# Decode steps in another order: three a slot in the later slots, words first in a step, two tiny loads issued first

## The chip, the cores and the metric

The kernel runs on one core of one Trainium2 chip. The metric is device time in microseconds (us) of one execution. Three executions of the kernel before took 1134.91, 1138.04 and 1139.94 us; the median is 1138.04 us. The profiled execution took 1136.57 us, of which 1134.7 us lie between its first and its last instruction.

## The reference

An attention block feeds two expert blocks, all in float32:

```
scores = q @ k^T / sqrt(64) + bias(distance, head), kept on the last 96 keys and the first 8
x  = softmax(scores) @ v                 # 4 x 8 heads x 768 x 64  ->  3072 x 512
h  = ((x @ w1) * (x @ w2)) @ w3          # 512 -> 1024
x2 = h @ w_out                           # 1024 -> 512
h2 = x2 @ w_in                           # 512 -> 2048
out = (h2 * cos(h2)) @ w_out2            # 2048 -> 512
```

`n_local` (96) and `n_global` (8) come as 64-bit integers, and the weights come as 64-bit words, so that each weight has to be decoded into float32 on the chip before it can be used.

## The kernel before, in words

The work runs in three stretches on one instruction stream per engine; the order is written out by hand in the code, and each engine takes its instructions in that order.

**Decoding a weight.** A weight piece of 128x512 values is loaded as 512 KB of 64-bit words into a `raw` buffer (`w_load`, L325, on SyncE's queue, called SP). Then ScalarE (ACT) makes two conversions, the "words" (`dec_words`, L338 and L339), and VectorE (DVE) makes a shift (`dec_shift`, L343), a sign (`dec_sign`, L347) and a sum (`dec_sum`, L355; the sum reads `raw` for the last time). Pieces of w1 and w2 are then split into a high part by a cast on ACT (`w_hi`, L419) and a low part on DVE (`w_lo`, L423). Pieces of w_in make seven combinations each pair (`combos`), and pieces of w_out2 are stored to DRAM (`late_w`, L359) for later. The pieces stand in one list of 72: 16 of w3 and w_out in turn, 24 of w3, w1 and w2, 16 of w_in and 16 of w_out2. The generator `decoder()` goes through that list one piece a step and stops (`yield`) after nearly each DVE operation; `decode(n)` runs it on by n stops. So `decode` calls, spread over the code of the other work, set where decoding stands in each engine's queue. The first 30 pieces ("fast") use six raw buffers, the later ones three.

**Start and chunks.** The start issues the first loads, computes the bias tables (`biases`, from `n_local` and `n_global`, which ACT's queue loads into `nraw`), and then 16 chunks multiply w3 with w_out into W (`wmm`, L890, float32 products) while the first attention units run: scores (L582), maximum with bias (`a_max`, L610), exponential (`a_exp`, L621), normalizing (`a_norm`, L631, L634, then L640 on ACT or L642 on GpSimd), transposes (L649, L651), a copy of them (L659, L664), values (`a_values`, L676).

**Slots.** Then 8 x 12 slots follow. Each runs one attention unit, 14 units ahead, and 24 products of the first expert block in two halves of 12 (L432): in the first eight slots of twelve the products with w1 and w2 (`up`), in the last four the products with W (`down`), whose result a slot later goes through one buffer, x2t (`down_out` L748, one buffer; `down_store` L751). Every third slot starts with the values of three units, whose v tile was loaded one slot earlier (`a_load_v`, L551).

**Second block.** After the slots the second expert block runs from the stored pieces; it has no decoding.

SP's queue takes its DMAs in the order of the code. A load into a raw buffer waits there until the sum that last read this buffer is done, and everything behind it on SP waits too.

Of the kernel before, what the change touches and what calls it, by code (L numbers as in the profile page):

```python
# [269 lines left out]
def fused(ctx, tc, a_qk, a_v, w3p, wo1p, w1p, w2p, winp, wo2p, n_global, n_local, out):  # L270
# [269 lines left out]
    def a_load_plain(n, queue=None):  # L540

        if not 0 <= n < PLAIN:
            return
        t = plain[n] = attn.tile([128, QK_W], F32R, tag="hh", name="hh")[0:64].bitcast(F32)
        (queue or nc.sync).dma_start(out=t, in_=a_qk[n, 0:64])
# [235 lines left out]
    with tc.manual_schedule():  # L781
# [8 lines left out]
        for o in "3A3A3A3A3A3A3A3ABBBBBBBB":  # L790
# [3 lines left out]
            else:  # L794
                n, m = ups.pop(0)
# [7 lines left out]
        tp = pool("tp", 1, side="right")  # L803
        EARLY = 30
# [6 lines left out]
        def decoder():  # L811


            n = len(dec)
            for i in range(2):
                w_load(*dec[i][:2])
            for i in range(n + 5):
                fast = i < EARLY
                k = [dec[i - l][0] if 0 <= i - l < n else None for l in range(5)]

                def ready(stage, lag):

                    for l in range(4, lag - 1, -1):
                        if k[l] and (stage, k[l]) not in done:
                            done.add((stage, k[l]))
                            if stage == "sum" or k[l] in xs and isinstance(dest[k[l]], str):
                                yield k[l]

                if fast and i + 2 < EARLY:
                    w_load(*dec[i + 2][:2])  # L830
                if k[0] and fast:
                    dec_words(k[0])
                if k[1]:
                    dec_shift(k[1])
                    yield
                for key in ready("sum", 2):
                    dec_sum(key)
                    yield
                for key in ready("hi", 3 if fast else 2):
                    w_hi(key, dest[key])  # L840
                for key in ready("lo", 4 if fast else 2):
                    w_lo(key, nc.vector)
                    yield
                if k[1]:
                    dec_sign(k[1])
                    yield
                if not fast:
                    for key in ready("sum", 1):
                        dec_sum(key)
                        yield  # L850
                    if k[1] and k[1][0] == "in" and k[1][1] % 2:
                        yield from combos(k[1][1] // 2)
                if EARLY <= i + 2 < n:
                    w_load(*dec[i + 2][:2])
                if k[0] and not fast:
                    dec_words(k[0])

        dest = {key: d for key, _, d in dec}
        done = set()
# [3 lines left out]
        def decode(n):  # L863
            for _ in range(n):
                next(steps_left, None)

        a_load_plain(0, nc.scalar)
        a_scores(0)
        nc.vector.memset(pt_ps, 0.0)
        steps_b = biases(tp)  # L870
        next(steps_b)
        make_identity(nc, ident)
        nv = dists = None
        for i in range(21):
# [9 lines left out]
        for c, (h, k) in enumerate(chunks):  # L884
            n = c - 1 if c < 2 * M1 - 1 else -9
            if k == 0:
                W_ps = {m: p_mm.tile([128, 512], F32, tag="mm", name="mm") for m in range(4)}

            def wmm(m):
                nc.tensor.matmul(  # L890
                    W_ps[m], lhsT=wt["w3", c][:, m * 128:(m + 1) * 128], rhs=wt["wo1", k],
                    start=k == 0, stop=k == M1 - 1,
                )
                if k == M1 - 1:
                    t = wt["W", 4 * h + m] = wts.tile(
                        [128, 2, 512], F32R, tag="Wb" if h else "Wa", name="W", bufs=4
                    )
                    nc.scalar.copy(out=t[:, 0, :], in_=W_ps[m])
                    nc.vector.tensor_tensor(
                        out=t[:, 1, :], in0=W_ps[m], in1=t[:, 0, :].bitcast(F32), op=ALU.subtract  # L900
                    )

            a_load(n + 3)
            a_load_v(n + 1 if n >= 0 else -1)
            if c < 4:
                bias_heads(*dists, range(2 * c, 2 * c + 2))
            elif c == 4:
                tp.release()
            if n > 0:
                a_scores(n)  # L910
            if n >= 0:
                a_load_plain(n + 2)
            a_values(n - 2)
            a_max(n)
            if c == 2 * M1 - 1:
                for m in range(4):
                    wmm(m)
            decode(1)
            a_out(n - 2)
            a_split_hi(n + 2)  # L920
            a_exp(n)
            decode(1)
            a_split_lo(n + 2)
            if c < 2 * M1 - 1:
                wmm(0)
                wmm(1)
            if c in (2, 3):
                wmm(2)
                wmm(3)
            a_transpose(n - 1)  # L930
            a_tcopy(n - 1)
            a_norm(n, True, lambda: decode(1)) if n >= 0 else decode(2)
            decode(2 if c < 8 else {14: 1, 15: 5}.get(c, 3))
            if not (c in (2, 3) or c == 2 * M1 - 1):
                wmm(2)
                wmm(3)
# [18 lines left out]
        def stage_tile():  # L955
            return wts.tile([128, 2, TB2], F32, tag="wA", name="x2f")
# [52 lines left out]
        for j in range(NB1):  # L1009
            for i in range(UPB):  # L1010
                sl = j * UPB + i
                n = sl + LEAD
                last = j == NB1 - 1
                if last and i == 0:
                    attn.release()
                    x2cA = pool("x2cA", 1)
                    x2_pool.update({k: x2cA for k in ("B11", "T2", "T1", "T3", "B21", "B22")})
                a_load(n + 3)
                if last:
                    if i == 0:  # L1020
                        x2_loads(0)
                        late_load(0)
                    elif i == 1:
                        late_load(1)
                        r0, r1 = stage_tile(), stage_tile()
                        nc.sync.dma_start(out=r0, in_=x2_cols("B12", 0))
                        x2_now = x2_steps(r0, r1)
                    elif i == 2:
                        late_load(2)
                    elif 3 <= i < 9:  # L1030
                        piece_load(0, i - 3)
                    if i == 7:
                        late_load(3)
                    if 8 <= i:
                        late_store(i - 8)
                a_scores(n)
                a_load_plain(n + 2)
                if (n - 2) % TPB == TPB - 1:
                    for u in range(n - 1 - TPB, n - 1):
                        a_values(u)  # L1040
                if n > LEAD + 1:
                    a_load_v(n - 1)
                a_split_hi(n + 2)
                if 1 <= i <= M1:
                    up_mult(j, i - 1)
                    up_hi(j, i - 1)
                a_max(n)
                decode(2)
                if i == 0 and j > 0:
                    down_out(j - 1, MO - 1)  # L1050
                    down_store(j - 1, MO - 1)
                elif i > M1:
                    down_out(j, i - M1 - 1)
                    down_store(j, i - M1 - 1)
                if 1 <= i <= M1:
                    up_lo(j, i - 1)
                a_exp(n)
                a_out(n - 2)
                a_split_lo(n + 2)
                if i < M1:  # L1060
                    up(j, i, "a")
                    up_copy(j, i)
                else:
                    down(j, i - M1, 0)
                a_transpose(n - 1)
                a_tcopy(n - 1)
                a_norm(n, sl < 8)
                decode(2 if sl < 8 or sl >= 48 else 1)
                if last and 2 <= i < 10:
                    some(x2_now, 1)  # L1070
                if i < M1:
                    up(j, i, "b")
                else:
                    down(j, i - M1, 1)
                if last and 2 <= i < 10:
                    some(x2_now, 1)
                if last and 6 <= i < 10:
                    run(late_split(i - 6))
# [214 lines left out]
        for q in range(NQ):  # L1293
            prev = None
            for k in range(NP):
                n = 2 * NP * q + k - 2
# [4 lines left out]
            for b in range(NP + 1 if last else NP):  # L1301
                n = 2 * NP * q + NP - 2 + b
# [119 lines left out]
```

## Time and profile before

| | |
|---|---|
| median of three executions | 1138.04 us |
| profiled execution | 1136.57 us |
| its span | 1134.7 us |
| TensorE (PE) busy | 1106.8 us, 98% |
| VectorE (DVE) busy | 777.9 us, 69% |
| ScalarE (ACT) busy | 680.2 us, 60% |
| chain that ended last, share of PE | 88% |

PE is busy nearly all the time, so that time can only go where PE has none to do or runs at a lower clock. The page shows the busy share in 40 slices of 28.4 us; PE is below nine tenths only in the first slice (5) and the last (7). The granted clock of PE is 0.995 of full speed on average. A wait of DVE, ACT or SP matters only where PE waits for what comes out of it.

### The profile page before, as it was taken

The numbers are of one execution on the slowest core, as the hardware profiler recorded it, in microseconds if no ns is written. First come the engines' busy times: TensorE is split into PE (matmuls) and PEld (weight loads), VectorE is DVE, ScalarE is ACT, GpSimd is POOL, SyncE is SP. The second block draws the span as 40 slices with busy tenths as digits, with TensorE's granted clock in tenths as the row PEclk, the third lists the DMA queues.
The fourth block names the chain that finished last, engine by engine and source line by source line (L and its number), as shares of the span: only waits on it lengthen the run. The fifth ranks groups of instructions, "written<-read, shape, count | busy, mean of one in ns | idle before, by whom it ended". The sixth has DMA issues, their size and how long they took to land.

```text
span 1134.7 us, 17350 instructions
## 1 busy us (share of the span) xinstructions
PE 1106.8 (98%) x6034; PEld 957.3 (84%) x6034; DVE 777.9 (69%) x1661; ACT 680.2 (60%) x1370; POOL 81.5 (7%) x161
## 2 busy tenths in 40 slices
PE   5999999999999999999999999999999999999997
PEld 2455899999999999999999878888888888888886
DVE  7797666757667676896516588885677884777741
ACT  6897776756666666866624476654355562555531
POOL 0000001111111112122100001100000000000000
PEclk9899999999999999999999999999999999999999
DMA  8865355554555555776254736549375459474261
GB/s 279 250 223 162 123 183 168 176 170 160 178 159 165 189 178 186 265 244 204 59 176 140 274 128 233 213 167 367 129 299 189 136 197 381 152 283 167 75 234 65
DMA packets 86768, 219.22 MB, mean 193 GB/s; under 512 B 9616, under 2 KB 26256, under 8 KB 86672
## 3 DMA queue, kind: packets, MB, share of 16 engines
q1 hardware_dynamic: 86160, 217.70, 56.0%
q8 instruction: 50, 0.82, 0.3%
q14 instruction: 46, 0.38, 0.1%
q10 hardware_dynamic: 512, 0.32, 0.1%
HBM read 178.14 MB, written 39.85 MB: 192 GB/s over the span
## 4 chain that ended last, share of the span: by engine, by line
PE 88%; DVE 6%; ACT 3%; DMA 2%; issue 1%; ACTq 0%; SPq 0%; DVEq 0%
PE mm L432 32%; PE o_ps L432 23%; PE h_ps L432 19%; PE x_ps L676 4%; PE mm L890 4%; PE pt_ps L649 2%; PE pt_ps L651 1%; PE s_ps L594 1%; PE s_ps L590 1%; PE s_ps L582 1%; DVE x L347 1%; DMA nraw<-in_n_global 1%; DVE x L355 1%; DMA raw<-in_w3p 1%; DMA v<-in_a_v 1%
## 5 line engine op out<-in xcount | busy, mean ns | idle before, releaser
L432 PE MATMUL o_ps<-o,g 128*128 128x512 f32 x960 | 223.3, 389 | 0.0
L432 PEld LDWEIGHTS o_ps<-o,g 128*128 128x128 f32 x960 | 180.0, 188 | 37.5
L432 PE MATMUL mm<-xT,wA 128*128 128x384 f32 x768 | 148.5, 343 | 0.0
L432 PE MATMUL mm<-ab,W 128*128 128x384 f32 x768 | 147.1, 341 | 0.0
L432 PE MATMUL mm<-xT,wB 128*128 128x384 f32 x768 | 147.1, 341 | 0.0
L432 PE MATMUL h_ps<-T,piece 128*128 128x512 f32 x576 | 141.7, 389 | 0.1
L432 PEld LDWEIGHTS mm<-xT,wA 128*128 128x128 f32 x768 | 133.1, 190 | 2.2 <-issue 1.5
L432 PEld LDWEIGHTS mm<-ab,W 128*128 128x128 f32 x768 | 131.6, 188 | 2.7 <-issue 2.4
L432 PEld LDWEIGHTS mm<-xT,wB 128*128 128x128 f32 x768 | 131.7, 188 | 2.1 <-issue 2.1
L432 PEld LDWEIGHTS h_ps<-T,piece 128*128 128x128 f32 x576 | 107.9, 188 | 23.2 <-DVE gr L1234 0.5
L558 ACT CAST hh<-qk 128x720 fp32r<-128x720 f32 x74 | 58.8, 794 | 104.1 <-PE s_ps L594 95.9
L642 POOL TENSOR_SCALAR e<-e,st 128x232 f32<-128x232 f32 x148 | 74.5, 516 | 498.9 <-DVE st L634 438.4
L432 PE MATMUL h_ps<-B,piece 128*128 128x512 f32 x432 | 106.0, 389 | 0.0
L432 PEld LDWEIGHTS h_ps<-B,piece 128*128 128x128 f32 x432 | 81.0, 188 | 17.1 <-DVE vv L1234 0.4
L621 ACT ACTIVATE e<-e,top 128x232 f32<-128x232 f32 (+1 forms) x192 | 89.1, 466 | 3.4 <-DVE top L610 3.3
L610 DVE CUSTOM_DVE_ANT_0 e<-s_ps,bias 128x232 f32<-128x232 f32 (+1 forms) x192 | 65.2, 376 | 32.9 <-PE s_ps L594 28.5
L1126 ACT ACTIVATE r<-r 128x1024 f32<-128x1024 f32 x48 | 51.0, 1062 | 33.3 <-DVE r L1120 33.3
L890 PE MATMUL mm<-wo,w 128*128 128x512 f32 x128 | 64.5, 638 | 4.8 <-DVE wo L355 4.8
L719 DVE TENSOR_TENSOR a_sb<-mm,a_sb 128x384 f32<-128x384 f32 x64 | 35.5, 554 | 46.5 <-PE mm L432 46.3
L1120 DVE SCALAR_TENSOR_TENSOR r<-kt,r 128x1024 f32<-128x1024 int32 x48 | 58.8, 1225 | 1.5
L659 ACT COPY pt<-pt_ps 128x512 f32<-128x512 f32 x80 | 46.7, 584 | 14.0 <-PE pt_ps L651 14.0
L1139 ACT CAST g<-gr 128x512 fp32r<-128x512 f32 x48 | 29.0, 621 | 42.1 <-PE o_ps L432 42.1
(136 smaller groups left out, 1681.5 us busy)
## 6 DMA issues: line engine op xcount, KB each, us to landing
piece<-a_s SPq DMA_DIRECT2D x84, 512.0 KB, 5.6
o<-o2s SPq DMA_DIRECT2D x80, 512.0 KB, 5.8
qk<-in_a_qk SPq DMA_DIRECT2D x74, 360.0 KB, 3.3
a_s<-ap SPq DMA_DIRECT2D x56, 256.0 KB, 2.3
v<-in_a_v SPq DMA_DIRECT2D x96, 128.0 KB, 3.1
raw<-in_w3p SPq DMA_DIRECT2D x16, 512.0 KB, 5.6
raw<-in_winp SPq DMA_DIRECT2D x16, 512.0 KB, 4.3
raw<-in_wo2p SPq DMA_DIRECT2D x16, 512.0 KB, 4.6
```

The lines of the kernel that those rows point to most:

```text
L432: nc.tensor.matmul(ps, lhsT=l, rhs=r, start=first and i + e == 0, stop=last and i == n - 1 and e == 2, skip_group_check=more,)
L558: nc.scalar.copy(out=hh[n], in_=qk_raw[n])
L610: nc.vector.tensor_tensor_reduce(out=es[n][:, e, :w], in0=sp[:, e, :w], in1=bias[:, 2 * p + e, :], scale=-0.125, scalar=3.0e38, op0=ALU.ad ...
L621: nc.scalar.activation(es[n][:, e, :w], es[n][:, e, :w], ACTF.Exp, bias=top[:, n, e:e + 1], scale=-1.0, accum_out=sts[n][:, 0, e:e + 1],)
L642: nc.gpsimd.tensor_scalar(x, x, st[:, 1, e:e + 1], 1.0, ALU.mult, ALU.mult)
L659: nc.scalar.copy(out=pts[n].rearrange("p a b c -> p (a b c)"), in_=pt_ps.rearrange("p a b c -> p (a b c)"),)
L676: nc.tensor.matmul(x[e * 64:(e + 1) * 64, i * 128:(i + 1) * 128], lhsT=vt[:kk, c, e * 64:(e + 1) * 64], rhs=pt[:kk, e, c, :], start=c == 0 ...
L719: nc.vector.tensor_tensor(out=t, in0=mm_ps.pop("b"), in1=t, op=ALU.mult)
L890: nc.tensor.matmul(W_ps[m], lhsT=wt["w3", c][:, m * 128:(m + 1) * 128], rhs=wt["wo1", k], start=k == 0, stop=k == M1 - 1,)
L1120: nc.vector.scalar_tensor_tensor(out=self.r, in0=self.kt, scalar=-c, in1=self.h if c == C1 else self.r, op0=ALU.mult, op1=ALU.add,)
L1126: nc.scalar.activation(self.r, self.r, ACTF.Sin, scale=0.5)
L1139: nc.scalar.copy(out=t[:, 0, :], in_=src[:, m, :])
```

## The change

The change is in `decoder()` and in the places that call it.

- In each step the load of the piece two further on and the words of the step's own piece now come first, before the shift of the piece before; in the steps after the thirtieth they came last. The load still needs the raw buffer whose last reader is the sum in the same step, a few operations further on.
- The low part of a w1 or w2 piece comes three steps after its words, not two, in the later steps.
- In the first three steps the sum follows its sign at once.
- The two tiny loads of `n_local` and `n_global` are issued on ACT's queue before the first attention load, not after it.
- The last chunk makes two stops of decoding, not five; slots from the 49th on make three, not four.

```diff
-                if fast and i + 2 < EARLY:
+                if i + 2 < n and fast == (i + 2 < EARLY):
                     w_load(*dec[i + 2][:2])
-                if k[0] and fast:
+                if k[0]:
                     dec_words(k[0])
                 if k[1]:
                     dec_shift(k[1])
...
-                for key in ready("lo", 4 if fast else 2):
+                for key in ready("lo", 4 if fast else 3):
                     w_lo(key, nc.vector)
                     yield
                 if k[1]:
                     dec_sign(k[1])
                     yield
-                if not fast:
+                if not fast or i <= 2:
                     for key in ready("sum", 1):
                         dec_sum(key)
                         yield
-                    if k[1] and k[1][0] == "in" and k[1][1] % 2:
-                        yield from combos(k[1][1] // 2)
-                if EARLY <= i + 2 < n:
+                if not fast and k[1] and k[1][0] == "in" and k[1][1] % 2:
+                    yield from combos(k[1][1] // 2)
+                if fast and i + 2 >= EARLY:
                     w_load(*dec[i + 2][:2])
-                if k[0] and not fast:
-                    dec_words(k[0])
...
+        steps_b = biases(tp)
+        next(steps_b)
         a_load_plain(0, nc.scalar)
         a_scores(0)
         nc.vector.memset(pt_ps, 0.0)
-        steps_b = biases(tp)
-        next(steps_b)
...
-            decode(2 if c < 8 else {14: 1, 15: 5}.get(c, 3))
+            decode(2 if c < 8 else {14: 1, 15: 2}.get(c, 3))
...
-                decode(2 if sl < 8 or sl >= 48 else 1)
+                decode(2 if sl < 8 else 1)
```

DVE's queue at the start, before. Here w3_135 and wo1_140 are the first two weight pieces, and nlo to nval are the small operations that read the two tiny loads.

```order
L343 TENSOR_SCALAR w3_135<-w3_135 128x512
L347 SCALAR_TENSOR_TENSOR w3_135<-raw_129,w3_135 128x512
L343 TENSOR_SCALAR wo1_140<-wo1_140 128x512
L355 ISA w3_135<-raw_129,w3_135 128x1024
L347 SCALAR_TENSOR_TENSOR wo1_140<-raw_131,wo1_140 128x512
L449 CAST nlo_156<-nraw_122 128x2
L450 CAST nhi_157<-nraw_122 128x2
L451 TENSOR_SCALAR nneg_158<-nlo_156 128x2
L452 TENSOR_TENSOR nhi_157<-nhi_157,nneg_158 128x2
L453 SCALAR_TENSOR_TENSOR nval_159<-nhi_157,nlo_156 128x2
L343 TENSOR_SCALAR w3_135<-w3_135 128x512
L355 ISA wo1_140<-raw_131,wo1_140 128x1024
```

The same place with the change:

```order
L343 TENSOR_SCALAR w3_135<-w3_135 128x512
L347 SCALAR_TENSOR_TENSOR w3_135<-raw_129,w3_135 128x512
L355 ISA w3_135<-raw_129,w3_135 128x1024
L343 TENSOR_SCALAR wo1_140<-wo1_140 128x512
L347 SCALAR_TENSOR_TENSOR wo1_140<-raw_131,wo1_140 128x512
L449 CAST nlo_156<-nraw_116 128x2
L450 CAST nhi_157<-nraw_116 128x2
L451 TENSOR_SCALAR nneg_158<-nlo_156 128x2
L452 TENSOR_TENSOR nhi_157<-nhi_157,nneg_158 128x2
L453 SCALAR_TENSOR_TENSOR nval_159<-nhi_157,nlo_156 128x2
L355 ISA wo1_140<-raw_131,wo1_140 128x1024
L343 TENSOR_SCALAR w3_135<-w3_135 128x512
```

Each of the two sums has moved ahead of the shift that stood before it; the small operations stand where they stood.

ACT's queue from the last cast of W (the end of the chunks) into the first slot, before. The L621 is the exponential of unit 14, and the L640 makes what the transposes of the second slot read.

```order
L898 CAST W_935<-mm_580 128x512
L419 CAST wB_938<-x_888 128x512
L338 ACTIVATE x_945<-raw_886 128x512
L339 ACTIVATE raw_886<-raw_886 128x512
L419 CAST wB_949<-x_916 128x512
L338 ACTIVATE x_956<-raw_914 128x512
L339 ACTIVATE raw_914<-raw_914 128x512
L419 CAST wB_960<-x_945 128x512
L621 ACTIVATE e_972,st_973<-e_972,top_87 128x232 x2
L715 COPY a_sb_993<-mm_980 128x384
L659 COPY pt_999<-pt_ps_90 128x512
L640 ACTIVATE e_972<-e_972,st_973 128x232 x2
```

The same place with the change:

```order
L896 CAST W_942<-mm_580 128x512
L338 ACTIVATE x_949<-raw_873 128x512
L339 ACTIVATE raw_873<-raw_873 128x512
L419 CAST wB_953<-x_875 128x512
L338 ACTIVATE x_973<-raw_916 128x512
L339 ACTIVATE raw_916<-raw_916 128x512
L419 CAST wB_977<-x_918 128x512
L621 ACTIVATE e_967,st_968<-e_967,top_87 128x232 x2
L715 COPY a_sb_995<-mm_982 128x384
L659 COPY pt_1001<-pt_ps_90 128x512
L640 ACTIVATE e_967<-e_967,st_968 128x232 x2
```

One cast fewer stands between W and the exponential, and the words right ahead of it belong to a later piece, the one in raw_916.

SP's queue in down slots with w_out2 pieces, before. L325 is the load of a w_out2 piece, late_w the store of one, qk and v the attention loads of a slot, x2s the store of x2t.

```order
L551 DMA v<-in_a_v 128x256
L325 DMA raw<-in_wo2p 128x1024
L751 DMA x2s<-x2t 128x384
L359 DMA late_w<-x 128x512
L325 DMA raw<-in_wo2p 128x1024
L537 DMA qk<-in_a_qk 128x720
L551 DMA v<-in_a_v 128x256
```

Such slots with the change:

```order
L537 DMA qk<-in_a_qk 128x720
L551 DMA v<-in_a_v 128x256
L325 DMA raw<-in_wo2p 128x1024
L751 DMA x2s<-x2t 128x384
L359 DMA late_w<-x 128x512
L537 DMA qk<-in_a_qk 128x720
L551 DMA v<-in_a_v 128x256
```

Each slot now has one load and one store of a piece, in slots 67 to 82 of 96, where before up to two of each fell into slots 61 to 73. The load now waits for the sum whose result the store behind it takes, and x2s stands between them.

## Rows read from the trace of the kernel before

**Rows 1.** The page's first part: busy time of each engine.

```profile
PE 1106.8 (98%) x6034; PEld 957.3 (84%) x6034; DVE 777.9 (69%) x1661; ACT 680.2 (60%) x1370; POOL 81.5 (7%) x161
```

**Rows 2.** PE's waits over the span: total, times, longest.

```profile
PE pt_ps L649 <- ACT e L640: 4.6, 2, 2.4
PE x_ps L676 <- DMA v<-in_a_v: 4.2, 3, 1.8
PE x_ps L676 <- ACT pt L659: 0.6, 2, 0.4
```

**Rows 3.** PE in order of time: start, length, work, idle before it.

```profile
28.17 0.53 PE L649 MATMUL pt_ps<-ident,e 128*128 128x128 f32 x2 [2.20 <-ACT e L640]
...
88.48 1.05 PE L582 MATMUL s_ps<-hh 64*128 64x232 f32 x4
...
94.12 1.05 PE L582 MATMUL s_ps<-hh 64*128 64x232 f32 x4
...
114.89 0.33 PE L649 MATMUL pt_ps<-ident,e 128*128 128x128 f32 x1 [2.43 <-ACT e L640]
...
115.53 3.84 PE L432 MATMUL mm<-xT,wA 128*128 128x384 f32 x12
...
478.70 0.66 PE L676 MATMUL x_ps<-pt,v 128*64 128x128 f32 x8 [1.18 <-DMA v<-in_a_v]
...
515.52 0.66 PE L676 MATMUL x_ps<-pt,v 128*64 128x128 f32 x8 [1.83 <-DMA v<-in_a_v]
516.12 2.37 PE L432 MATMUL mm<-ab,W 128*128 128x384 f32 x12
```

**Rows 4.** Stretches: engines' busy time, then PE's clock, DMA share, GB/s.

```profile
100.00:110.00 10.00, 9.98 (x44) 7.04 (x42) 8.07 (x17) 7.33 (x14) 0.00 (x0) 1.00 0.29 98
110.00:120.00 10.00, 7.57 (x33) 6.69 (x32) 7.33 (x21) 6.50 (x17) 0.00 (x0) 0.83 0.52 172
...
510.00:520.00 10.00, 8.16 (x64) 7.63 (x63) 5.45 (x16) 7.24 (x18) 1.15 (x2) 1.00 0.90 327
```

**Rows 5.** ACT's queue, DVE and ACT in order of time at the start.

```profile
1.97 0.45 ACTq L441 DMA_DIRECT2D nraw<-in_n_global  x1
...
10.35 0.17 DVE L449 CAST nlo<-nraw 128x2 f32<-128x2 int32 x1 [1.54 <-DMA nraw<-in_n_global]
...
15.13 0.42 DVE L343 TENSOR_SCALAR w<-w 128x512 int32<-128x512 int32 x1
...
13.71 0.67 ACT L338 ACTIVATE w<-raw 128x512 f32<-128x512 f32 x1 [1.08 <-DMA raw<-in_w3p]
```

**Rows 6.** DVE, then ACT, from the chunks' end into the slots.

```profile
103.52 2.48 DVE L899 TENSOR_TENSOR W<-mm,W 128x512 fp32r<-128x512 f32 x4 [0.61 <-ACT W L898]
...
107.23 0.69 DVE L355 CUSTOM_DVE_ANT_0 x<-raw,x 128x1024 uint16<-128x1024 uint16 x1
...
102.93 2.00 ACT L898 CAST W<-mm 128x512 fp32r<-128x512 f32 x4
...
112.37 0.49 ACT L621 ACTIVATE e<-e,top 128x232 f32<-128x232 f32 x1 [1.08 <-DVE top L610]
...
115.12 0.65 ACT L338 ACTIVATE x<-raw 128x512 f32<-128x512 f32 x1
...
116.26 0.60 ACT L419 CAST wB<-x 128x512 fp32r<-128x512 f32 x1
```

**Rows 7.** The raw tiles' DMAs from 78 to 125 us, issue to landing.

```profile
DMA to landing us min/median/max: 3.4/3.7/5.0
```

**Rows 8.** DMA issues from 470 to 526 us: count, size, median to landing.

```profile
v<-in_a_v SPq DMA_DIRECT2D x9, 128.0 KB, 4.5
x2s<-x2t SPq DMA_DIRECT2D x4, 192.0 KB, 3.9
```

**Rows 9.** SP's queue and ACT in order of time, w_out2 slots.

```profile
474.07 0.38 SPq L551 DMA_DIRECT2D v<-in_a_v  x1
...
511.56 0.48 ACT L748 COPY x2t<-mm 128x384 f32<-128x384 f32 x1 [2.88 <-DMA x2s<-x2t]
```

## The prediction

> **What bounds the kernel now.** I read the page's busy line first: PE is busy 1106.8 of 1134.7 us [rows 1], so that only the missing 28 us can move, plus what PE does at its lower clock. The second view is PE's list of waits: it waits 4.6 us in two pieces for normalized exponentials, 4.2 us in three pieces for v tiles, and 0.6 us for copies of transposes [rows 2]. The third is PE in order of time, which says where: 2.20 us at 28 us, 2.43 us at 114.89, and the v waits between 478.70 and 515.52 [rows 3]. The first wait belongs to the start, the second to the change from chunks to slots, the last three to the slots that decode w_out2. The fourth view is the table of stretches: the granted clock is 0.83 in the stretch of the 2.43 us wait, a mixture of the two levels, and 1.00 in that of the 1.83 us wait [rows 4]. Twelve products right after the first wait take 3.84 us, right after the second 2.37 [rows 3]; so the wait at 114.89 costs 2.43 + 1.47 us. Everything else is PE at work, and the second block does not change.
>
> **Start.** DVE is through with the second piece's sign at 10.35 − 1.54 = 8.81, and then idles until 10.35 for the tiny load of n_global, which ACT's queue issued third, at 1.97 [rows 5]. Issued second, behind an issue of some 0.6 us, it leaves about 0.6 us earlier. The sums that have moved are as many as before. DVE is then in one unbroken run of bias and decode steps that ends in the wait of 2.20 us on PE, so what DVE gains there PE gains. The gain can't be more than 0.75 us: the third piece's words start at 13.71 because ACT waits for its DMA, they take 0.67, and the shift that reads them started at 15.13 [rows 5], so beyond 15.13 − 14.38 DVE would wait again. From the other side, the tiny transfers now run beside the first two weight loads, and if these land later nothing is gained; I put that end at −0.5, as much lost as could be gained. I take +0.4, below the 0.6 of the issue. PE's first scores, whose load is now third, are early enough: PE has the 2.20 us to spare behind them.
> The Trainium skill speaks against this edit ("DMA: Bandwidth & Descriptors", section "Queues, rings and completion order"): each DMA engine takes turns between the rows of SP and ACT, packet by packet, and keeps the order in a row. By it, the 256 tiny descriptors hold up the weight loads sooner and the attention load altogether; no row here separates the two. By it alone the term is 0, and the sum 0.4 less.
>
> **Chunks to slots.** The last wait before the slots' rhythm hangs on this chain: casts of W on ACT from 102.93, low parts of W on DVE until 103.52 + 2.48 = 106.0, nine decode operations, then the maximum and ACT's exponential at 112.37 and, 2.52 us later, PE at 114.89 [rows 3, 6]. The change takes three of the nine away, so the maximum would come more than 2 us earlier. But another wait steps in. ACT now has the words of raw_916 in front of the exponential, and that load may be issued only when the sum behind the low parts of W has released its buffer. I work it out: a 0.52 us cast stands in place of a pair of words of 1.14 us (115.12 to 116.26) ahead of the casts of W, which thus start 0.6 us earlier, and the low parts end near 105.4. Sign and sum take some 0.7 each (0.69 for the sum at 107.23): release at 106.8. A raw load lands after 3.4 to 5.0 us [rows 7]; the DMA share is only 0.29 in the stretch before [rows 4], so I take 3.4: 110.2. Words and a cast take 1.14 + 0.52, and then the 2.52 us to PE's start: 114.4, less 0.2 because DVE no longer makes the exponential's successor wait for a sum. PE starts at 114.2, not 114.89: the wait is 1.7 to 1.8 us, not 2.43. This is nearest to the 1.83 us that left the clock at 1.00, so I count the 1.47 us too: +2.1. Bounds: with both gone entirely +3.9; with 5.0 us for the landing PE starts 0.9 later than before, −0.9.
> The Trainium skill ("DMA: Bandwidth & Descriptors", section "Anatomy of one DMA — SWDGE (gpsimd) path") fits a DMA with 2.0 us plus bytes by 436 GB/s, 3.2 us for 512 KB by my estimate; the rows have 3.4 as their least, and the measurement decides. By the page the sum would be 0.2 better.
>
> **First slots.** The words now come a whole step before their shift, so DVE no longer stands between them. The 0.6 us of waits for copies of transposes [rows 2] should go; I count +0.5, with 0 to 0.9 as ends. In the chunks from the twelfth on, ACT meets loads that are issued at a sum and read one step later. A chunk takes 5.6 us (scores at 88.48 and 94.12 [rows 3]) and has seven stops, a step four: 3.2 us. With 3.7 us for a load [rows 7] ACT waits about 0.5 us now and then. I cost that at nothing, since the exponentials run ahead of their transposes there: both waits for them lie elsewhere, at 28.17 and 114.89 [rows 2, 3]. If that cover goes, it is the last rival below.
>
> **w_out2 slots.** The three v waits are 4.2 us. In that stretch a slot's DMAs go out in a burst when DVE ends its sum: v leaves at 474.07, lands after 4.5 us in the median, at 478.6, and PE starts at 478.70 [rows 3, 8, 9]. With three stops a slot DVE has a decode operation less in each, so the burst goes out about 1 us earlier against PE, and that is nearly the 1.18 us of this wait. In the slots with up products I expect none. In the four slots with x2t, however, SP now holds the store of x2t behind a load that waits for the slot's sum. The store lands 3.9 us after that [rows 8]; the next copy into x2t needs its buffer, and ACT has the exponential behind that copy: 511.56 waited 2.88 us for just this [rows 9]. One turn is 0.5 (issue) + 3.9 + 0.4 (copy) + 1.0 (exponential) + 1.0 (normalizing and sum) = 6.8 us against some 5.1 us of PE in such a slot (twice 2.37 and some 0.4). So DVE falls behind by 1.7 us a slot, 5 us in three turns, less 1.5 for the values in one of them. The v load issued at the end of that comes late once; I put this one wait at 2.0 us, near the longest seen, 1.83. So +2.2; ends: +4.2 (no wait) and −1.5 (three such waits, or one of 5.7).
>
> **Sum.** 0.4 + 2.1 + 0.5 + 2.2 = 5.2 us off the profiled execution's 1136.57 us: 1131.4. The median of the three runs is 1.5 us above that execution, so by it 1132.8. I say 1132.
>
> **Rivals.**
> 1. Every wait goes: start +0.75, chunks to slots +3.9, first slots +0.9, v +4.2, 9.8 us off: 1127 to 1128. For it: the decode work in front of each critical operation is less. Against: the two waits for DMAs above follow from the order on ACT and SP and from durations in the rows.
> 2. The waits only change their name: PE is released at 114.7 or later and the clock falls as before, the x2t turn gives back the v waits. Then the start and the first slots remain, 1 us: 1136 to 1137. For it: my 114.2 is only 0.7 from 114.89, and 1.8 us lies between a wait that left the clock alone and one that did not. That the edits do nothing at all is this same time.
> 3. Slower: loads that are issued only at a sum land in 5.0 us or more, not 3.4 to 3.7. From the twelfth chunk three loads take part in a turn of three steps, and each third one adds 5.0 − 3.2 = 1.8 us: 4.8 us over eight loads, of which I let half be covered by the lead of the exponentials; the first slot's wait grows by 0.9 and keeps its clock loss; and the x2t turn with 5.4 us grows to 8.3, three turns 9.6 behind, some 6 to 8 us in v waits in place of 4.2. In all 2.4 + 0.9 + 3, less the 1 us of the start and the first slots: 5.3 to 6 us more, about 1142 to 1143. It decides from a landing of about 4.5 us on. For it: the longest raw load of rows 7 is 5.0. Against: the median is 3.7.
>
> **How the numbers follow.** Forecast (1129.5 to 1135) 0.52; rival 1 0.15; rival 2 0.22; rival 3 0.11. The range that leaves out half of rival 1 and rival 3 is 1127 to 1139. Half a per cent, about what can be told from no change, is 5.7 us: faster means below 1132.3. That takes all of rival 1 and a little over half of the forecast, 0.43; the same takes the rest of the forecast and rival 2, 0.46; slower is rival 3, 0.11.
>
> **What would show it.** In the profile after, DVE's first read of the tiny loads comes before 10.35 and PE's wait near 28 us starts and ends earlier by up to 0.75. In the first slot ACT idles ahead of words for a raw load, not ahead of the exponential for DVE, and PE's wait there is 1 to 2 us at a clock near 1.00. No v wait stands in the w_out2 slots but one behind the four x2t slots, after an ACT wait for x2s. Wrong would be a wait of PE in the last chunks, a clock of 0.83 after the wait, or v waits in several slots; then the second or third rival holds.

## The result: slower, 1146.29 us

Seven runs of the changed kernel have a median of 1146.29 us (1141.96 to 1148.01), seven of the kernel before 1138.04; the ratio is 1.0065, with a 95% interval of 1.0043 to 1.0087. The forecast was 1132 us, with a range that ended at 1139. The profiled execution took 1141.96 us, of which 1140.0 are its span; it is the shortest of the seven, so its trace shows the least of the loss. A second profile, below, shows a part of the rest.

PE's list of waits in the changed kernel answers to [rows 2]. Columns: who waited at which line for what; us in total, times, longest. Its first row is left out, as it is in [rows 2]: at the start PE waits 11.4 us for attention loads, where before it waited 7.0 us for them and 4.8 us for the first sum.

```profile
PE pt_ps L649 <- POOL e L642: 6.8, 5, 1.7
PE pt_ps L649 <- ACT e L640: 4.4, 2, 2.4
PE x_ps L676 <- DMA v<-in_a_v: 2.0, 1, 2.0
PE x_ps L676 <- ACT pt L664: 1.1, 1, 1.1
PE x_ps L676 <- ACT pt L659: 0.6, 1, 0.6
```

The three v waits have become one of 2.0 us, as forecast. New is the first line, which no step of the forecast has: five waits for normalized exponentials that GpSimd makes. The timeline of PE says where they are (its rows answer to [rows 3]).

```profile
115.24 0.33 PE L649 MATMUL pt_ps<-ident,e 128*128 128x128 f32 x1 [1.99 <-ACT e L640]
...
115.81 2.35 PE L432 MATMUL mm<-xT,wA 128*128 128x384 f32 x12
...
188.76 0.33 PE L649 MATMUL pt_ps<-ident,e 128*128 128x128 f32 x1 [1.19 <-POOL e L642]
...
514.16 0.66 PE L676 MATMUL x_ps<-pt,v 128*64 128x128 f32 x8 [0.63 <-ACT pt L659]
...
524.02 0.33 PE L649 MATMUL pt_ps<-ident,e 128*128 128x128 f32 x1 [1.69 <-POOL e L642]
...
531.03 0.33 PE L649 MATMUL pt_ps<-ident,e 128*128 128x128 f32 x1 [1.47 <-POOL e L642]
...
537.47 0.66 PE L676 MATMUL x_ps<-pt,v 128*64 128x128 f32 x8 [1.98 <-DMA v<-in_a_v]
```

The wait of the first slot is 1.99 us and the twelve products behind it take 2.35, so the clock stayed up; 188.76 is one of three such places (the others are 324.21 and 459.85), where PE waits in the up slots right behind those with x2t. The other two of the five waits, 524.02 and 531.03, lie in the w_out2 slots. Why GpSimd is late stands on SP, and then on ACT, between 181 and 189 us:

```profile
181.69 0.33 SPq L325 DMA_DIRECT2D raw<-in_winp  x1
182.11 0.38 SPq L751 DMA_DIRECT2D x2s<-x2t  x1
```

```profile
177.30 0.48 ACT L748 COPY x2t<-mm 128x384 f32<-128x384 f32 x1 [1.62 <-DMA x2s<-x2t]
...
186.23 0.48 ACT L748 COPY x2t<-mm 128x384 f32<-128x384 f32 x1 [4.91 <-DMA x2s<-x2t]
186.60 0.49 ACT L621 ACTIVATE e<-e,top 128x232 f32<-128x232 f32 x1
```

The copy that ended at 177.78 could have been stored at once. Its store stands behind a load that waits for the slot's sum, and goes out at 182.11; ACT sits idle for 4.91 us until it has landed, and has the exponential behind the next copy; normalizing follows at 188.25, and PE waits 1.19 us. Over the whole span the list of those who wait for the store of x2t has one row, first the kernel before, then the changed one:

```profile
  ACT x2t L748: 4.4, 2
```

```profile
  ACT x2t L748: 31.1, 10
```

A table adds the places up. It gives the start of the values (x_ps, L676) in PE's timeline, less that of the kernel before, at the same instruction. "Loads last", "counts only" and the rest are the experiments below.

| at (before) | changed | loads last | counts only | hold, w_in | hold, w_out2 |
|---|---|---|---|---|---|
| 158.94, after the first slots | −2.28 | −2.28 | −2.75 | −1.44 | −1.48 |
| 192.58 | −0.50 | −2.28 | −2.75 | +0.39 | −1.48 |
| 326.27 | +1.29 | −2.28 | −2.75 | +2.16 | −1.47 |
| 459.97 | +3.21 | −2.28 | −2.75 | +4.33 | −1.48 |
| 512.81 | −0.16 | −5.65 | −6.12 | +0.99 | −4.84 |
| 581.48, slots over | +5.07 | −7.71 | −8.18 | −1.08 | +0.15 |

In the changed kernel three steps of 1.8 to 1.9 us (5.5 in all) lie in the slots that decode w_in. A step is longer than its wait in the list, 1.2 us: behind 188.76 the transposes take 0.63 us, not 0.35, and the rest lies in shorter gaps. Then 3.4 us of v waits go, and 5.2 us come back before the slots end. The second block adds 0.2.

### The profile page after: what moved, and what is told of

The parts are those of the page before. It is cut to its first block, busy times and chain, and to the rows that moved or that the text cites. A ratio compares the mean times of both kernels' runs of the same rounds, so it can differ in the third digit from the quotient of the medians.

```text
span 1140.0 us, 17321 instructions
## 1 busy us (share of the span) xinstructions
PE 1107.1 (97%) x6034; PEld 955.3 (84%) x6034; DVE 774.3 (68%) x1661; ACT 677.5 (59%) x1370; POOL 78.9 (7%) x161
## 4 chain that ended last, share of the span: by engine, by line
PE 83%; DMA 6%; ACT 5%; DVE 3%; issue 2%; SPq 0%; POOL 0%; ACTq 0%; POOLq 0%
PE mm L432 29%; PE o_ps L432 23%; PE h_ps L432 19%; DMA x2s<-x2t 3%; PE x_ps L676 3%; PE mm L888 3%; PE pt_ps L649 2%; ACT e L621 2%; PE pt_ps L651 1%; PE s_ps L594 1%; PE s_ps L582 1%; PE s_ps L590 1%; DMA raw<-in_w3p 1%; ACT raw L339 1%; DMA raw<-in_w2p 1%
## 5 line engine op out<-in xcount | busy, mean ns | idle before, releaser
L642 POOL TENSOR_SCALAR e<-e,st 128x232 f32<-128x232 f32 x148 | 71.8, 496 | 507.0 <-DVE st L634 449.2
L621 ACT ACTIVATE e<-e,top 128x232 f32<-128x232 f32 (+1 forms) x192 | 89.3, 468 | 1.4 <-DVE top L610 1.3
L649 PE MATMUL pt_ps<-ident,e 128*128 128x128 f32 x192 | 46.7, 277 | 11.2 <-POOL e L642 6.8
```

Source lines behind the costliest of these rows:

```text
L621: nc.scalar.activation(es[n][:, e, :w], es[n][:, e, :w], ACTF.Exp, bias=top[:, n, e:e + 1], scale=-1.0, accum_out=sts[n][:, 0, e:e + 1],)
L642: nc.gpsimd.tensor_scalar(x, x, st[:, 1, e:e + 1], 1.0, ALU.mult, ALU.mult)
L649: nc.tensor.transpose(pt_ps[:, e, 0, :], e_t[:, e, :128], ident)
```

## Experiments

All comparisons are with the kernel before on the same chip, in five rounds; its medians there were 1136.2 to 1136.7 us. Where two experiments from different chips are set against each other, differences below half a us say nothing.

**Loads last.** The changed kernel with the late loads behind their sum again.

```diff
-                if i + 2 < n and fast == (i + 2 < EARLY):
+                if fast and i + 2 < EARLY:
...
-                if fast and i + 2 >= EARLY:
+                if EARLY <= i + 2 < n:
```

> The changed kernel with one line group undone: in the steps after the thirtieth the load of a weight piece stands at the end of the step again, behind its sum; words still come first, the counts of stops and the start stay changed. Theory (the load that waits for its sum holds SP, so that the store of x2t behind it, ACT's next copy into x2t and the exponential behind that copy come late): the x2t copies no longer wait for x2s (31.1 us in 10 waits now, some 4 us before), PE's idle time returns to below 1 us in the stretches at 180, 320 and 440 us (3.7 us now) and by about 5 us at 520 to 540 us; the span falls from 1140.0 to about 1131, the time to 1133, and no runs with a granted clock of 0.990 are left. First rival (three stops a slot give the normalizing too late a place, whatever SP does): the waits for GpSimd's e in the w_out2 slots stay, 5 us or more, and the time stays above 1138. Second rival (the words in front are what delays the exponential): the three waits in the w_in slots stay.

Measured: 1130.35 us, ratio 0.9946 (0.9933 to 0.9958), span 1127.4. The waits for GpSimd and for v are gone from PE's list, and the wait for the store is small. Who waits for it:

```profile
  ACT x2t L748: 1.7, 1
```

So the place of the load is worth 15 us of the median (1145.03 us for the changed kernel on this chip, below), and both rivals fall. The time is 2.7 us below the 1133 that I expected.

**Store on ACT's queue.** The loads stay where the change put them.

```diff
-        nc.sync.dma_start(out=x2s[m, :, j * TB:(j + 1) * TB], in_=x2t.pop((j, m)))
+        nc.scalar.dma_start(out=x2s[m, :, j * TB:(j + 1) * TB], in_=x2t.pop((j, m)))
```

> The changed kernel with its loads where the change put them; only the store of x2t is issued on ACT's queue instead of SP's, so that no load stands in front of it. Theory: as if the load were moved, no x2t copy waits more than 2 us, PE's idle time falls by 8 to 9 us less some tenths for 32 issues on ACT: span about 1131 to 1132, time 1133 to 1134. Rival (the load's late landing itself, hence late words, is what holds ACT): ACT still waits as long, now for raw ahead of words, and the time stays within 2 us of 1142.

Measured: 1133.93 us (1130.92 to 1136.58), ratio 0.9977 (0.9966 to 0.9988), span 1129.4; no wait for GpSimd's e is left. With the load still held by the sum, taking only the store out of its way gives back most of the loss. It is 3.6 us worse in the median than moving the load, 2.0 in the span. ACT now issues the store itself, which takes it 0.33 us, and 17 times it sat idle 0.4 us between the copy and the exponential; that this is what costs the rest is not shown, since PE's timeline keeps up with loads last until 512.81 and loses 1.4 us behind it. Copies of x2t still waited 11.0 us in three waits, against my bound of 2 each, but the longest, 6.8 us, lies in the second block.

**Hold, w_in** and **hold, w_out2.** The load ahead of its sum only up to the third piece of w_out2, or only from the fourth on (`>=` in place of `<`).

```diff
-                if i + 2 < n and fast == (i + 2 < EARLY):
+                held = not fast and i + 2 < 59
+                if i + 2 < n and (held or fast and i + 2 < EARLY):
...
-                if fast and i + 2 >= EARLY:
+                if EARLY <= i + 2 < n and not held:
```

> The changed kernel with the load ahead of the sum only for the pieces up to the third of w_out2 (those that are loaded in the chunks and in the w_in slots); the loads of the later w_out2 pieces stand behind their sum. Theory: the three places near 185, 320 and 455 us, where a load meets a slot with x2t, cost 1.8 to 1.9 us each as in the trace of the changed kernel, 5.5 us in all, and the w_out2 slots cost nothing: 1130.35 + 5.5 = 1135.9, with PE waiting for GpSimd's e there, three times 1.2 us. Rival (the delay of the w_in slots is made up by the time the w_out2 slots end, so that only those count): 1131 to 1132.

> The complement: the load ahead of the sum only for the w_out2 pieces from the fourth on. Theory: nothing is lost before 470 us, and from there to 580 us the 5.4 us that the kernel with its loads last gains on the kernel before turn into a loss of 1.9, 7.3 us in all: 1130.35 + 7.3 = 1137.6, up to 2 or 3 us more where the clock falls behind a wait. The forecast had 2.0 us of waits in this stretch (1132.4). Rival (the two stretches aggravate each other): both single kernels together lose less than 12 us, and the rest of the 15 us that the changed kernel lies above 1130.35 comes from having both.

Measured: 1135.54 us (0.9990, 0.9981 to 0.9999) and 1139.16 us (1.0020, 1.0011 to 1.0030). Above loads last that is 5.2 and 8.8 us, together 14.0 of the 15; the two expectations had 5.5 and 7.3, the second with up to 3 more for the clock. PE's waits in the first and in the second:

```profile
PE pt_ps L649 <- POOL e L642: 3.6, 3, 1.3
```

```profile
PE pt_ps L649 <- POOL e L642: 3.3, 2, 1.7
PE x_ps L676 <- DMA v<-in_a_v: 2.0, 1, 2.0
```

The two parts add up and hardly aggravate each other. The table shows that the w_in loss appears at the three places and stays, and the w_out2 loss between 512.81 and 581.48.

**Counts only.** The kernel before with two stops in the last chunk and three from the 49th slot on.

```diff
-            decode(2 if c < 8 else {14: 1, 15: 5}.get(c, 3))
+            decode(2 if c < 8 else {14: 1, 15: 2}.get(c, 3))
...
-                decode(2 if sl < 8 or sl >= 48 else 1)
+                decode(2 if sl < 8 else 1)
```

> The kernel before with the counts of stops alone changed: the last chunk makes two, slots from the 49th on three. The forecast's theory for the w_out2 slots (a decode operation less in each slot sends the burst of DMAs out about 1 us earlier, so that the v tiles land in time): the three v waits of 4.2 us shrink to below 1.5 us, and the time falls by 2 to 3 us to about 1133.5. Rival (what removed the v waits in the kernel with its load last, 1130.35 us, is that words stand first in a step): two or three v waits are left, 3 us or more, and the time stays within 1 us of 1136.4. For the change from chunks to slots the forecast's theory (three operations fewer ahead of the maximum) expects PE's wait near 115 us to end 1 to 2 us earlier than 114.89; the rival that the words are what counts there expects no move.

Measured: 1129.02 us, ratio 0.9938 (0.9924 to 0.9951), the lowest of all: 7.2 us less, where I expected 2 to 3. No v wait is left. The first two rows are PE's at the first slot, where the wait of 2.43 us [rows 3] and the lower clock are gone; the third is the values at 490.20.

```profile
112.19 0.33 PE L649 MATMUL pt_ps<-ident,e 128*128 128x128 f32 x1 [0.19 <-ACT e L640]
...
112.76 2.36 PE L432 MATMUL mm<-xT,wA 128*128 128x384 f32 x12
...
490.20 1.32 PE L676 MATMUL x_ps<-pt,v 128*64 128x128 f32 x20
```

SP's issue of the v tile that these values read last:

```profile
486.40 0.44 SPq L551 DMA_DIRECT2D v<-in_a_v  x1
```

It leaves 3.80 us ahead of the values. In the kernel before the pair was this (PE, then SP), 2.57 us apart:

```profile
494.88 0.88 PE L676 MATMUL x_ps<-pt,v 128*64 128x128 f32 x12
496.96 0.66 PE L676 MATMUL x_ps<-pt,v 128*64 128x128 f32 x8 [1.21 <-DMA v<-in_a_v]
```

```profile
492.31 0.38 SPq L551 DMA_DIRECT2D v<-in_a_v  x1
```

So the burst goes out 1.2 us earlier against PE, where the forecast said about 1. The forecast overlooked that these transfers also land sooner: this tile after 3.3 us, not 4.5, and in the median from 470 to 526 us after 3.8, not 4.5 [rows 8].

What the counts alone do not remove are the waits for copies of transposes in the first slots; they grow from 0.6 us [rows 2] to:

```profile
PE x_ps L676 <- ACT pt L659: 2.4, 2, 1.3
```

**Counts back.** Loads last, and the old counts.

```diff
-            decode(2 if c < 8 else {14: 1, 15: 2}.get(c, 3))
+            decode(2 if c < 8 else {14: 1, 15: 5}.get(c, 3))
...
-                decode(2 if sl < 8 else 1)
+                decode(2 if sl < 8 or sl >= 48 else 1)
```

> The changed kernel with its late loads at the end of a step again, and the counts of stops as before too (five in the last chunk, four from the 49th slot on); what is left of the change are words first, the low parts a step later, the first sums at once and the start. Theory of the counts: the v waits come back, 3 to 4 us, and the time is about 1134, 3 to 4 us above the same kernel with the new counts (1130.35). Theory of the words: it stays within 1 us of 1130.35.

Measured: 1139.97 us, ratio 1.0036 (1.0024 to 1.0048), more than expected: the counts are worth 9.6 us here, and without them what is left of the change is 3.7 us slower than the kernel before. PE's rows, of which the first includes a wait of 3.77 us at 117.34, ahead of the first slot's products:

```profile
PE pt_ps L649 <- ACT e L640: 7.2, 2, 3.8
PE x_ps L676 <- DMA v<-in_a_v: 4.7, 3, 2.5
```

What is left of the change, with the old counts, makes the first slot later than in the kernel before (117.34 against 114.89, 1.2 us of it from a later start), and does nothing for the v waits.

**Hold only.** The kernel before with the load ahead of its sum, words last, counts as before.

```diff
-                if fast and i + 2 < EARLY:
+                if i + 2 < n and fast == (i + 2 < EARLY):
...
-                if EARLY <= i + 2 < n:
+                if fast and i + 2 >= EARLY:
```

> The kernel before with one part of the change alone: in the steps after the thirtieth the load stands at the start of a step, ahead of the sum that it waits for; words stay last, the counts stay. Theory (the hold of SP is what costs, and it needs nothing else): x2t copies wait for x2s some 20 to 30 us in all, PE idles 1.2 to 1.8 us more at each place where a w_in load meets a slot with x2t (two or three places) and more in the w_out2 slots; the time rises by 4 to 8 us to 1140 to 1144. Rival (the hold costs only because the words in front make the exponential wait for a load): the time stays within 1.5 us of 1136.4.

Measured: 1170.18 us, ratio 1.0293 (1.0279 to 1.0307), +34 us where I expected 4 to 8. The hold needs no help, but x2t is not the greater part of it (17.7 us in six waits). PE now waits seven times for v:

```profile
PE x_ps L676 <- DMA v<-in_a_v: 19.3, 7, 4.0
```

What SP's loads wait for sums, in the kernel before, in the changed one and with the hold only:

```profile
SPq L325 <- DVE x L355: 35.5, 11, 6.0
```

```profile
SPq L325 <- DVE x L355: 124.1, 33, 5.9
```

```profile
SPq L325 <- DVE x L355: 149.7, 37, 6.3
```

With four stops a slot, load and sum no longer fall into the same slot each time, and the v tile of the slot stands behind the load as well. The trace shows the second half of this: in all seven cases the v load leaves 0.8 to 1.0 us behind a load that had waited for its sum, and lands 3.7 to 5.8 us later. One of them, first the sum on DVE, then SP, then the values on PE:

```profile
439.35 0.69 DVE L355 CUSTOM_DVE_ANT_0 x<-raw,x 128x1024 uint16<-128x1024 uint16 x1
440.07 0.33 SPq L325 DMA_DIRECT2D raw<-in_wo2p  x1
...
440.97 0.38 SPq L551 DMA_DIRECT2D v<-in_a_v  x1
444.84 0.66 PE L676 MATMUL x_ps<-pt,v 128*64 128x128 f32 x8 [0.98 <-DMA v<-in_a_v]
```

The granted clock is 0.980 in this trace, 0.995 before, and 0.83 from 520 to 540 us, so products behind the waits ran slower as well. That the spread over two slots is why v is hit I read from the order of the code; no run separates it.

**Tiny loads first.** The kernel before with that edit alone.

```diff
+        steps_b = biases(tp)
+        next(steps_b)
         a_load_plain(0, nc.scalar)
         a_scores(0)
         nc.vector.memset(pt_ps, 0.0)
-        steps_b = biases(tp)
-        next(steps_b)
```

> The kernel before with one edit alone: the two tiny loads are issued ahead of the first attention load. The forecast's reason: DVE reads the tiny loads 0.2 to 0.6 us earlier and PE's wait near 28 us ends earlier, -0.4. Theory now: the tiny transfers push the landing of the first attention load (4.6 to 8.8 us in the trace of the changed kernel) and of the first weight loads; ACT's first words start 1.5 to 2 us later than at 4.40, the first products after the start about 0.3 later, the wait at 28 us gets longer and the products behind it run at the lower clock for longer: about 0.9 us later at the end of the start, time about 1137.5 for a profile, a difference that only the trace tells.

Measured: 1136.86 us, ratio 1.0008 (0.9999 to 1.0016): no difference. DVE does not idle any more ahead of the tiny loads, but reads them at 10.60, not 10.35, since the first words on ACT wait for their load:

```profile
6.21 0.66 ACT L338 ACTIVATE w<-raw 128x512 f32<-128x512 f32 x1 [2.69 <-DMA raw<-in_w3p]
```

In the kernel before they did not:

```profile
4.40 0.66 ACT L338 ACTIVATE w<-raw 128x512 f32<-128x512 f32 x1 [0.67 <-DMA raw<-in_w3p]
```

The attention load that now stands behind the tiny ones takes longer from issue to landing; before, then with this edit (KB, us):

```profile
hh<-in_a_qk ACTq DMA_DIRECT2D x1, 180.0 KB, 4.6
```

```profile
hh<-in_a_qk ACTq DMA_DIRECT2D x1, 180.0 KB, 8.7
```

DVE is 1 us later at 28 us, and PE's wait there grows from 2.20 to 3.42 us. Yet the scores behind the next eight products start 0.5 us earlier than before (38.57, not 39.07), because these products ran at the higher clock for longer (4.94 us, not 5.54). I expected 0.9 later.

**Loads last, attention load first.** Loads last with the start undone (the edit above, reversed).

> The changed kernel with its late loads at the end of a step again and the attention load first at the start, as before. Theory (the order at the start does not show in the time, since the end of the start moves with the clock's rise by more than with the loads): within 1 us of 1130.35. Rival (the two tiny loads in front cost the 0.9 us by which the first trace of the changed kernel was late at 39 us): about 1129.3, and PE's wait near 28 us is back at 2.2 us or less.

Measured: 1129.82 us, ratio 0.9944 (0.9931 to 0.9958), and 2.6 us for the wait near 28 us. That is no difference from 1130.35 that these runs can tell, and neither can the start alone be told from nothing.

**The changed kernel again.**

> The changed kernel once more, unaltered. Its seven runs fell in two groups, about 1142.5 us at a granted clock of 0.995 to 0.996 and about 1146.3 at 0.990 to 0.992; the trace is of the first. Theory: the second group has the same waits, but PE's clock falls behind one or more of the new waits of 1.5 to 2.0 us (at 180 to 200, 320 to 340, 440 to 460 or 520 to 540 us), each costing about 1.5 us as at 114.89 us in the kernel before; a trace at 0.990 would show stretches below 1.00 just there. Rival: the lower clock comes in a stretch without waits, as in the second block; then it is no effect of the change's waits, and the kernel before should show such runs as well.

Measured: 1145.03 us, ratio 1.0075 (1.0062 to 1.0088); its trace is of a run of 1142.78 us at a granted clock of 0.992. Two stretches of the first trace, then the same of this one (us, busy time of PE, PEld, DVE, ACT and POOL, granted clock of PE, DMA share, GB/s):

```profile
110.00:120.00 10.00, 8.01 (x52) 6.57 (x52) 6.25 (x21) 8.06 (x21) 0.00 (x0) 1.00 0.50 167
...
520.00:540.00 20.00, 14.86 (x100) 13.05 (x100) 13.28 (x38) 12.80 (x33) 3.46 (x6) 1.00 0.67 205
```

```profile
110.00:120.00 10.00, 8.22 (x37) 6.59 (x37) 6.26 (x18) 8.81 (x23) 0.00 (x0) 0.83 0.47 142
...
520.00:540.00 20.00, 16.36 (x102) 14.73 (x101) 13.36 (x38) 12.54 (x31) 3.46 (x6) 0.91 0.66 207
```

The clock did fall behind two of the waits in this run and not in the first, about 1 and 1.5 us each by the products behind them:

```profile
114.50 0.33 PE L649 MATMUL pt_ps<-ident,e 128*128 128x128 f32 x1 [1.78 <-ACT e L640]
...
115.07 3.42 PE L432 MATMUL mm<-xT,wA 128*128 128x384 f32 x12
...
531.77 0.33 PE L649 MATMUL pt_ps<-ident,e 128*128 128x128 f32 x1 [1.61 <-POOL e L642]
...
532.40 3.89 PE L432 MATMUL mm<-xT,wA 128*128 128x384 f32 x12
```

At the w_in places it did not fall. That explains little of the spread: this run is only 0.8 us longer than the first trace's, since the v wait behind the second of these waits shrinks from 1.98 to 0.45 us (PE, 538.21); a run of 1144.32 us had a clock of 0.995, and no trace of a run above 1142.78 exists. Where the rest of those runs goes stays open.

## Why the prediction was wrong, by its steps

**The step that failed is the turn of x2t**, as the prediction put it: "In the slots with up products I expect none. In the four slots with x2t, however, SP now holds the store of x2t behind a load that waits for the slot's sum." The mechanism was right, and the experiments with the store on ACT's queue and with the loads last show it. Its extent was wrong twice.

- It was looked for only in the w_out2 slots. The diff moves every load after the thirtieth step, and in six slots with x2t a load for w_in or the first of w_out2 stands there too, in pairs near 185, 320 and 455 us. The forecast had 0 there; 5.5 us in the trace, 5.2 us as a kernel of its own.
- In the w_out2 slots the forecast had 2.0 us of waits left out of 4.2. There are 5.8: 0.63, 1.69, 1.47 and 1.98. Its own working had DVE 5 us behind in three turns, less 1.5, and charged 2.0 of the 3.5 that remain, for no reason but that no longer wait had been seen; and it let only the v load come late at the end, with no term for the normalized exponentials that the same turns delay. PE met these first. The turns took 7.7, 9.0 and 7.0 us (SP's stores at 507.33, 515.07, 524.09 and 531.10), not 6.8. The longest is the one with the values, which the forecast counted as relief: between exponential and normalizing DVE there waits for ACT and makes the low parts of the values' result and of the next queries and keys.

```profile
521.11 0.56 DVE L691 TENSOR_TENSOR xT<-x_ps,xT 128x384 fp32r<-128x384 f32 x1 [4.71 <-ACT xT L690]
...
522.68 0.17 DVE L631 TENSOR_SCALAR st<-st 128x2 f32<-128x2 f32 x1
```

As a kernel of its own this part costs 8.8 us.

With the hold taken out, the forecast comes near: loads last is 6.0 us below the kernel before, where the sum without the 2.0 that it charged for the hold said 7.2. That is in part luck, since its terms miss in both directions, as the steps below show.

The third rival had the sign, a time near that of the profiled execution (1142 to 1143 for 1141.96; the median is 1146.29) and even the length of a turn (8.3), but its cause was the wrong one: raw loads that land late and stall the chunks from the twelfth on. Nothing of this showed: from 78 to 125 us they land after 3.8 us in the median, 3.7 before [rows 7], and PE is busy for at least 69.97 of the 70 us from 40 to 110 us in every trace.

**Start.** +0.4 forecast, 0 measured. The step "what DVE gains there PE gains" has the sign wrong on DVE: the tiny transfers delay the first weight loads by about 1.7 us (words at 6.12, not 4.40, in the changed kernel), and DVE ends 1 us later; in the first trace of the changed kernel PE is 0.9 us late from 40 us on, in the second 0.35. I had this as the other end, −0.5. The rule of the Trainium skill that the prediction weighed ("DMA: Bandwidth & Descriptors", section "Queues, rings and completion order") gave 0, and the runs agree with it: the attention load now lands 8.8 us behind its issue, not 4.6, and the time is the same.

**Chunks to slots and first slots.** The chain is the one forecast: the raw load leaves at the sum (107.76), and ACT idles ahead of its words.

```profile
111.27 0.66 ACT L338 ACTIVATE x<-raw 128x512 f32<-128x512 f32 x1 [2.92 <-DMA raw<-in_w1p]
```

PE starts at 115.24, though, not at 114.2: the casts of W come at 103.23, 0.3 us later than before and not 0.6 earlier, which fits the 0.9 us that the start lost. Its wait is 1.99, for 1.7 to 1.8, and the clock stayed up, so the step is worth 2.1 in this trace (from +0.92 at the values of 95.10 to −1.20 at those of 120.28). But that it is the forecast's 2.1 is luck. My reason for counting the clock ("nearest to the 1.83 us that left the clock at 1.00") does not hold: with words first and the new counts it stayed behind waits of 1.83 (store on ACT's queue), 1.99 and 2.08 us (hold, w_in) and fell behind 1.78 (second trace), 2.15 (loads last), 2.16 (hold, w_out2) and 2.60 us (attention load first). Where it fell, the step is worth 0.2 to 0.8, not 2.1. The first slots bring 1.1, more than the 0.5 forecast and its end of 0.9. In all the changed kernel is 2.3 us ahead at 158.94, where start, step and first slots had 3.0. And the words in front cost about what they gain: they end the waits for copies of transposes and bring the wait for the load; the counts alone are 2.75 ahead there.

**w_out2 slots, the stops.** Right: three stops send the v tiles out 1.2 us earlier and, with their earlier landing, end the v waits; the upper end had +4.2, and counts only gains 5.4 from 459.97 to 581.48. This gain is in the changed kernel too, under the loss.

So the parts of the change are: the counts, 7.2 us faster; the hold of SP, 15 us slower; words first, the low parts a step later and the start together, about 1 us slower with the new counts (1130.35 against 1129.02, on two chips, so hardly to be told from nothing) and 3.7 us slower with the old ones.

## What to carry to other kernels

An issue that waits in a queue can delay everything behind it there, as SP's loads delayed the stores of x2t here: before moving a load ahead of the operation that frees its buffer, list every DMA of every stage that then stands behind it, and who reuses those buffers. Do this for all places that the edited line reaches, not only for the stage in which the profile shows waits. Take stops out where a burst of transfers comes just too late: here two numbers were worth more than all reordering.

## What the runs showed of the hardware

The clock does not go by the length of one wait: behind 2.08 us (hold, w_in), 1.99 us (first trace) and 1.83 us (store on ACT's queue) in the first slot it stayed at 1.00, behind 1.78 us (second trace) the same products took 3.42 us, not 2.35. It stayed in the three traces in which PE came late from the start, by 0.9 to 1.6 us at 95.10, and fell in the others with words first and the new counts, by 0.35 us at most; why is open. And two DMAs of 1 KB each, issued ahead of one of 180 KB on the same queue, made it land 8.7 us behind its issue, not 4.6, and moved the first use of a 512 KB load on another queue from 4.40 to 6.21 us (tiny loads first, with nothing else changed).
